# Two token blocks of a rational layer interleaved by units, with the first two units in halves

## The chip, the core and the metric

The kernel runs on one core of a Trainium2 chip. The metric is the device time of one execution in microseconds (us). Its engines are TensorE (PE in the rows, with its weight loads as PEld), VectorE (DVE), ScalarE (ACT), GpSimd (POOL) and SyncE (SP), which issues most transfers.

## What is computed

Three layers on 3072 tokens (4 batches x 768) of width 384:

```python
y = attn(q, k, v, a_re, a_im)             # linear attention by a complex decaying state
x = y.transpose(0, 2, 1, 3).reshape(3072, 384)
h = x @ w_in                              # 384 -> 2048
P = a[0] + a[1]*h + a[2]*h*h + a[3]*h*h*h
Q = 1.0 + abs(b[0])*abs(h) + abs(b[1])*h*h
x = (P / (Q + 1e-06)) @ w_out             # 2048 -> 384
# routed layer: the best of 8 experts for each token, times its gate
out[mask] = gate_w[mask, None] * (relu(x[mask] @ w1[e]) @ w2[e])
```

All matrices are fp32.

## The kernel before

**Stages.** The recurrence takes the first 250 us or so; the rational layer lies from 254 to about 690 us, the routed layer from there to 930, then the last rows are scattered.

**The rational layer.** Tokens are cut into 8 blocks of 384, the 2048 hidden columns into 8 units of 256, two halves of 128. `unit(b, i)` does unit `i` of block `b`. Each fp32 operand is a high part rounded to fp32r plus the rest (`xh`, `xl`, `wi..0`, `wi..1`, `wo..0`, `wo..1`, `gh`, `gl`), and each product is three matmuls: high x high, low x high, high x low. So a unit has 18 matmuls on `w_in` (`mm1`, L1016, 9 for each half), into PSUM tile `ph0` or `ph1` (two banks each, one for each half), and 18 on `w_out` (`mm2`, L1061), into three accumulators of one bank, one for each 128 tokens, that run over all 8 units of the block. Between them lies the rational function: on ScalarE Abs (L1039), Square (L1040), a second Square of h (L1042), Ln (L1045), Exp (L1046) and the cast to `gh` (L1050), on VectorE four SCALAR_TENSOR_TENSOR (L1044, L1047 to L1049) and the low part `gl` (L1051). Abs, the Square of L1042 and the VectorE operation of L1044 read h from PSUM, so `ph` is free again after these three. The accumulators and the h of unit 2 of block 0 (in halves, since both `ph` are taken then) come from a pool of four banks (`acc`). That unit writes its two halves to two of them.

**Parts.** The weights are loaded early as `wfi`, `wfo` and split late: the high cast on VectorE (L208), the low part on GpSimd (L210). `xsplit(b)` makes `xh` and `xl` of a block (L227, L231), two blocks in turn.

**The routed layer** goes over slots of 256 gathered tokens with the same `ph` and `acc` tiles (L1016 for the first product, L1458 for the second, transposes of gathered rows L1373, weight casts and splits L1411, `gl` L1447). Small blocks for the rest of the tokens lie beside the later slots: their rows are gathered by GpSimd, transposed (L1545), multiplied by weights `mw` (L1560, L1570) and their results turned (L1564, L1578).

**The order of the work.** No queue is written out by hand. Every piece of work is handed to a `Plan` with its engine or engines, an assumed duration, what it reads and writes, and at times a due time. When the program is built, `Plan.emit` picks, piece by piece, the one that could start soonest by its own clock and is due first; `COST` and `LEAN` weigh the engines for pieces that two engines could take, `UNIT` and `GROUP` are the assumed times of a unit and a slot and set the due times with `LAG`, `RAMP`, `AHEAD`, `BEFORE` and `FETCH`. Each engine then runs its instructions in that fixed order, and waits come from the data.

Names of halves in the plan, as `("h", 2 * j + n)`, serve the plan alone. The waits in the program are set for the tiles that are allocated, `ph0` or `acc1`.

Of the kernel before, what the change touches and what calls it, by code (L numbers as in the profile page):

```python
# [9 lines left out]
F32 = mybir.dt.float32  # L10
# [109 lines left out]
def tile_recurrence_rational_moe(tc, q, k, v, a_re, a_im, w_in, w_out, ca, cb, emb, tau, w1, w2, cst_d, out):  # L120
    nc = tc.nc
    V, A, G, T, SY = nc.vector, nc.scalar, nc.gpsimd, nc.tensor, nc.sync

    with ExitStack() as top:
        top.enter_context(tc.manual_schedule())
        dram = top.enter_context(tc.tile_pool(name="dram", bufs=1, space=bass.MemoryType.DRAM))
        x2d = dram.tile([NT + 1, XC], F32, name="x2d")
        idl = [dram.tile([NID, 1], I32, name=f"idl{t}") for t in range(TPB)]
        safe = dram.tile([NT, WO], F32, name="safe")
        cp = top.enter_context(tc.tile_pool(name="cp", bufs=1))  # L130
        cst = cp.tile([P, C_N], F32, name="cst")

        def cc(o, n=1):
            return cst[:, o:o + n]

        def misc(i):
            return cc(C_MISC + i)

        ident = cc(C_ID, P)
        cnt = cp.tile([P, E], F32, name="cnt")  # L140
        V.memset(cnt, 0.0)

        with ExitStack() as run:
            xtp = run.enter_context(tc.tile_pool(name="xtp", bufs=1))
            xT = xtp.tile([P, KT, NT], F32, name="xT")
            wfp = run.enter_context(tc.tile_pool(name="wfp", bufs=1))
            hold = run.enter_context(tc.tile_pool(name="hold", bufs=1))
            parts = weight_parts(tc, hold, wfp)
            xs = input_parts(tc, hold, xT)
            bad = cp.tile([P, 3], I32, name="bad")  # L150
            coef = coefs(tc, ca, cb, tau, cp)

            def prepare(again):
                with ExitStack() as att:
                    attention(tc, att, q, k, v, a_re, a_im, w_in, w_out, emb, cst, cst_d, cc, misc, ident, hold, xT, bad, idl, x2d, coef, parts, xs, again)

            def layers(ctx, again):
                return mixture(tc, ctx, cst, cc, misc, ident, cp, hold, wfp, parts, xs, xT, cnt, idl, x2d, w1, w2, out, coef, bad, safe, again)

            prepare(False)  # L160
            with ExitStack() as first:
                rare, rest = layers(first, False)
                with tc.If(nc.values_load(rare, min_val=0, max_val=1) != 0):  # L163
                    rest()
            with tc.If(nc.values_load(bad[0:1, 0:1], min_val=0, max_val=1) != 0):
                xs.tiles.clear()
                prepare(True)
                sequential_attention(tc, q, k, v, a_re, a_im, cst, cc, ident, dram, xT, coef)
                for kk in range(KT):
                    xs.hi(nc.scalar, 0, kk)  # L170
                    xs.lo(nc.gpsimd, 0, kk)
                plain_rational(tc, coef, parts, xT, safe)
                with ExitStack() as second:
                    layers(second, True)[1]()

# [122 lines left out]

COST = {'A': 0.7094815, 'G': 0.3193946, 'V': 1.1, 'T': 0.0, 'S': 0.0}
LEAN = {'A': 0.1119026, 'G': 0.1802717, 'V': 0.4995443, 'T': 0.0, 'S': 0.0}  # L300
SPREAD = 0.0605191
EARLY_BY = -0.9788931
LEAN_FROM = 4.5359957
MOE = SimpleNamespace(price=COST, bias=LEAN, margin=EARLY_BY, start=LEAN_FROM, chain=0.0, warm=WINDOW, port=True, lat=0.13)
# [120 lines left out]
def attention(tc, ctx, q, k, v, a_re, a_im, w_in, w_out, emb, cst, cst_d, cc, misc, ident, hold, xT, bad, idl, x2d, coef, parts, xs, again):  # L425
# [511 lines left out]

def mixture(tc, ctx, cst, cc, misc, ident, cp, hold, wfp, parts, xs, xT, cnt, idl, x2d, w1, w2, out, coef, bad, safe, again):
    nc = tc.nc
# [3 lines left out]
    NQ = NF2 // 2  # L943
    UNIT, GROUP = 6.0000, 16.4000
    LAG = 6.0
    FIRST = 2
    DELAY = -0.4256865
    RAMP = 1.5
    LATER = 1.0
    AHEAD = 6.0  # L950
    BEFORE = 8.0
    FETCH = 0.0

# [15 lines left out]
    ub, ku = [*u, spared["gl3"]], [[("u", i)] for i in range(3)] + [[("gl", 3)]]  # L969
    hp = [ps.tile([P, 2, 512], F32, name=f"ph{i}") for i in range(2)]  # L970
    banks = [ps.tile([P, 512], F32, name=f"acc{i}") for i in range(4)]
    half = [hp[i][:, j, :] for j in range(2) for i in range(2)]
# [3 lines left out]
    add = lambda *a, due=1e9, **k: st.plan.add(*a, due=due + st.delay, **k)  # L976
    bank = lambda key: banks[st.plan.bank[key][1]]

    def copy(e, o, i):
        (A.copy if e == "A" else eng[e].tensor_copy)(o, i)  # L980
# [32 lines left out]
    def products(o, steps):  # L1013
        steps = list(steps)
        for n, (l, r) in enumerate(steps):
            T.matmul(o, l, r, start=(n == 0), stop=(n == len(steps) - 1))  # L1016

    def unit(b, i):
# [10 lines left out]
        due = UNIT * n + 2.94  # L1029
        if n == FIRST:  # L1030
            pieces = [(slice(j, j + 1), [("hu", j)], lambda j=j: bank(("hu", j))[:, :BLK].rearrange("p (o n) -> p o n", o=1)) for j in range(2)]
            for j in range(2):
                add(("T", 1.45), lambda e, j=j: mm1(bank(("hu", j))[:, :BLK], j), r=wkey("i", i) + xkey(b % 2), w=[("hu", j)], take=("C", ("hu", j)), due=due)
# [18 lines left out]
        for t in range(TPB):  # L1052
            key = ("acc", b, t)

            def mm2(e, t=t, key=key):
                o = bank(key)[:, :WO]
                sl = slice(t * P, (t + 1) * P)
                for j in range(2):
                    c = slice(j * WO, (j + 1) * WO)
                    for k, (x, y) in enumerate(((g, wh), (g, wl), (l, wh))):  # L1060
                        T.matmul(o, x[:, j, sl], y("o", i)[:, c], start=(i == 0 and j == 0 and k == 0), stop=(i == NP - 1 and j == 1 and k == 2))  # L1061

            add(("T", 0.98), mm2, r=kg + kl + wkey("o", i), w=[key], take=("C", key) if not i else None, due=UNIT * (n + LAG - max(4 - n, 0) * RAMP) + 0.997 * (t + 1))

# [11 lines left out]
    def route(b):  # L1076
# [16 lines left out]
        for t in range(TPB):  # L1093
            key = ("acc", b, t)
            add([("A", 0.46), ("V", 0.48)], lambda e, t=t, key=key: copy(e, spread()[t], bank(key)[:, :WO]), r=[key], w=[("row", t)] + over, give=key)
            if again:
                add(("S", 0.65), lambda e, t=t: SY.dma_start(rows[t], safe[b * BLK + t * P:b * BLK + (t + 1) * P, :]), w=[("row", t)], lat=1.8)
# [643 lines left out]
```

## Time and profile before

| | us |
|---|---|
| median of 3 runs | 949.84 (949.75 to 953.89) |
| the profiled execution | 952.94 |
| its span, first to last instruction | 951.2 |
| around the span | 1.7 |
| TensorE busy | 876.5 (92%) |
| VectorE busy | 738.4 (78%) |
| ScalarE busy | 704.6 (74%) |
| GpSimd busy | 239.5 (25%) |

The span is that of the one execution that was profiled, and the times in the rows below are from its start. Mean granted clock of TensorE over the span: 0.971 of 2.4 GHz. In a row of a timeline the number in brackets is the idle time of the engine just before the instruction, and what ended it.

### The profile page before, as it was taken

How to read it: one execution, taken by the hardware profiler on the slowest of the kernel's cores; microseconds unless marked ns; L12 is line 12 of the kernel's file. 1: busy time of each engine (PE TensorE's matmuls, PEld its weight loads, DVE VectorE, ACT ScalarE, POOL GpSimd, SP SyncE). 2: the span in 40 equal slices, each digit the busy share in tenths (PEclk: the TensorE clock that was granted, in tenths of full speed). 3: DMA queues.
4: the chain of work that ended last, by engine and by line, in shares of the span. 5: the costliest groups of instructions: out<-in, count | busy, mean ns of one | idle time of the engine just before them, and what ended most of it. 6: DMA issues, size and time to landing. Idle time of an engine off the chain costs nothing. (4 is left out here: it accounts for less than half of the span.)

```text
span 951.2 us, 16898 instructions
## 1 busy us (share of the span) xinstructions
PE 876.5 (92%) x6119; PEld 832.3 (88%) x6119; DVE 738.4 (78%) x1418; ACT 704.6 (74%) x1134; POOL 239.5 (25%) x184
## 2 busy tenths in 40 slices
PE   2999998989878999999999999999999979999991
PEld 2788987878778999999999999999999868889991
DVE  7989988989799879797978888796977875655610
ACT  7989998999586989888889888878653544555520
POOL 2425434546244110101000010102223143215400
PEclk9999999999889999999999999999999989999996
DMA  9987988784200000010100000123202166541500
GB/s 173 200 171 171 178 188 180 144 181 111 81 0 1 1 26 1 1 26 1 26 1 26 1 26 1 26 67 92 34 9 85 26 192 209 158 142 35 176 26 22
DMA packets 172873, 76.50 MB, mean 80 GB/s; under 512 B 140840, under 2 KB 167352, under 8 KB 172772
## 3 DMA queue, kind: packets, MB, share of 16 engines
q1 hardware_dynamic: 168804, 65.58, 30.5%
q0 software_dynamic: 3968, 9.66, 3.5%
q8 instruction: 52, 0.85, 0.4%
q14 instruction: 49, 0.40, 0.2%
HBM read 95.33 MB, written 9.96 MB: 111 GB/s over the span
## 5 line engine op out<-in xcount | busy, mean ns | idle before, releaser
L1016 PE MATMUL ph<-xh,wi 128*128 128x384 f32 (+1 forms) x1284 | 306.0, 317 | 8.4 <-DVE wfi L488 4.2
L1016 PEld LDWEIGHTS ph<-xh,wi 128*128 128x128 f32 x1284 | 223.7, 190 | 10.5 <-DVE wfi L488 4.4
L1061 PE MATMUL acc<-wo,gh 128*128 128x392 f32 x768 | 201.8, 344 | 4.1 <-ACT gh L1050 4.1
L1016 PE MATMUL ph<-xl,wi 128*128 128x384 f32 (+1 forms) x642 | 203.1, 316 | 0.0
L1061 PEld LDWEIGHTS acc<-wo,gh 128*128 128x128 f32 x768 | 141.1, 189 | 4.4 <-ACT gh L1050 4.4
L1061 PE MATMUL acc<-wo,gl 128*128 128x392 f32 x384 | 131.6, 343 | 2.5 <-DVE gl L1051 2.5
L1016 PEld LDWEIGHTS ph<-xl,wi 128*128 128x128 f32 x642 | 121.8, 190 | 0.0
L1124 POOL DMA_INDIRECT idl<-tok,pos x24 | 24.6, 1026 | 281.2 <-DVE pos L1121 177.4
L1061 PEld LDWEIGHTS acc<-wo,gl 128*128 128x128 f32 x384 | 72.6, 189 | 3.3 <-DVE gl L1051 3.3
L1458 PE MATMUL acc<-wo,gh 128*128 128x384 f32 x256 | 70.0, 355 | 3.4 <-DVE wo L1411 3.4
L1051 DVE TENSOR_TENSOR gl<-u,gh 128x768 fp32r<-128x768 f32 x48 | 47.0, 979 | 27.1 <-PE acc L1061 26.1
L1039 ACT ACTIVATE sq<-ph,quad 128x768 f32<-128x768 f32 x43 | 38.8, 902 | 30.2 <-PE ph L1016 27.3
L1446 ACT ACTIVATE gh<-ph 128x512 fp32r<-128x512 f32 x36 | 21.6, 599 | 48.7 <-PE ph L1016 33.4
L1415 POOL DMA_INDIRECT out_dram<-ah,ido x24 | 29.8, 1242 | 98.0 <-ACT ah L1463 54.9
L1458 PEld LDWEIGHTS acc<-wo,gh 128*128 128x128 f32 x256 | 45.8, 194 | 9.4 <-issue 4.9
L497 ACT COPY qkT<-bank 96x512 f32<-96x512 f32 x96 | 50.6, 586 | 2.0 <-PE bank L619 1.3
L628 PE MATMUL bank<-qkT 96*128 96x128 f32 x384 | 50.8, 280 | 1.2 <-ACT qkT L497 1.2
L1355 POOL DMA_INDIRECT xT<-x2d,ids x24 | 27.2, 1133 | 98.2 <-DVE oh L1102 45.9
L1044 DVE SCALAR_TENSOR_TENSOR u<-u,qtmp,ph 128x768 f32<-128x768 f32 x47 | 47.3, 1006 | 5.4 <-ACT u L1042 5.3
L618 PE MATMUL bank<-cst,qf 128*96 128x128 f32 x192 | 48.2, 290 | 3.2 <-ACT qkT L497 3.2
L628 PEld LDWEIGHTS bank<-qkT 96*128 96x128 f32 x384 | 47.0, 193 | 2.9 <-ACT qkT L497 2.7
L1047 DVE SCALAR_TENSOR_TENSOR sq<-sq,quad,ah 128x768 f32<-128x768 f32 x43 | 46.6, 1085 | 0.6 <-ACT ah L1046 0.5
(297 smaller groups left out, 2157.6 us busy)
## 6 DMA issues: line engine op xcount, KB each, us to landing
xT<-in_moe_w_dram SPq DMA_DIRECT2D x26, 1536.0 KB
mw<-in_moe_w_dram SPq DMA_DIRECT2D x32, 384.0 KB
raw<-in_moe_w_out_dram SPq DMA_DIRECT2D x16, 384.0 KB
raw<-in_moe_w_in_dram SPq DMA_DIRECT2D x16, 384.0 KB
x2d<-rows SPq DMA_DIRECT2D x24, 192.5 KB
a_re<-in_a_re_dram SPq DMA_DIRECT2D x24, 192.0 KB
a_im<-in_a_im_dram SPq DMA_DIRECT2D x24, 192.0 KB
k<-in_k_dram SPq DMA_DIRECT2D x24, 192.0 KB
```

The source lines that it names most:

```text
L497: (A.copy if e == "A" else eng[e].tensor_copy)(o, i)
L618: T.transpose(pv[:, i, 0, :], Q[:, 2 * j + i, :], ident)
L628: T.matmul(pb(b)[:, i * P:(i + 1) * P], O[:, i, 1, :], O[:, i, 0, :], start=True, stop=True)
L1016: T.matmul(o, l, r, start=(n == 0), stop=(n == len(steps) - 1))
L1039: add(("A", 0.81 if many else 0.45), lambda e, c=c, h=h: A.activation(z[:, c], h(), AF.Abs, scale=coef.kb), w=kh + kz_)
L1044: add(("V", 0.93 if many else 0.53), lambda e, c=c, h=h: V.scalar_tensor_tensor(out=w[:, c], in0=w[:, c], scalar=coef.d, in1=h(), op0=ALU. ...
L1047: add(("V", 0.93), lambda e: V.scalar_tensor_tensor(out=z, in0=z, scalar=coef.e, in1=s, op0=ALU.add, op1=ALU.mult), r=ks, w=kz_)
L1051: add(("V", 0.87), lambda e: V.tensor_tensor(out=l, in0=w, in1=g.bitcast(F32), op=ALU.subtract), r=kw + kg, w=kl, lat=0.27)
L1061: T.matmul(o, x[:, j, sl], y("o", i)[:, c], start=(i == 0 and j == 0 and k == 0), stop=(i == NP - 1 and j == 1 and k == 2))
L1355: G.indirect_dma_start(out=xg[i][t], out_offset=None, in_=x2d[0:n, :], in_offset=bass.IndirectOffsetOnAxis(ap=ids[i][:, t:t + 1], axis=0), ...
L1415: G.indirect_dma_start(out=out[:, :], out_offset=bass.IndirectOffsetOnAxis(ap=dst, axis=0), in_=src, in_offset=None, bounds_check=NT - 1, ...
L1458: T.matmul(o, x[:, j, sl], w[:, c], start=(q == 0 and j == 0 and n == 0), stop=(q == NQ - 1 and j == 1 and n == 2))
```

## The change

The units of blocks 0 and 1 are no longer done block after block. A list `PAIR` sets their order: units 0 to 2 of block 0, then a unit of block 1 and one of block 0 in turn, block 1 two units behind, then the rest of block 1. The units are counted along that list. The first two go through a new function `halves_of`, which does every step for each half of 128 columns by itself (L1032 for ScalarE and L1033 for VectorE in the changed program, casts L1043, `gl` L1044, matmuls on `w_out` L1051). Unit 2, and unit 16 of the list, hold h in two pool banks (`LOOSE`). Units 3 to 15 all hold h in the same tile, `ph0` (`hp[0]`), each half under a name of its own. Two blocks have six accumulators: four are pool banks, and two of block 1 lie in the two banks of the other `ph` (`AWAY`). Which bank pair is `ph` and which is the pool now follows the order in which the recurrence frees them (`order`); the second `ph` is named `ph2`, the pool banks `acc10`, `acc11`, `acc30`, `acc31`. `xsplit(1)` is handed in ahead of all units. The constants of the plan are other ones, for the whole of both layers.

```diff
-COST = {'A': 0.7094815, 'G': 0.3193946, 'V': 1.1, 'T': 0.0, 'S': 0.0}
+COST = {'A': 1.1052526, 'G': 0.0767626, 'V': 1.1, 'T': 0.0, 'S': 0.0}
...
+    free = [t for t, _ in sorted(plan.pools["B"], key=lambda x: x[1])]
+    return sorted(range(4), key=lambda p: max(free[2 * p:2 * p + 2]))
...
-    UNIT, GROUP = 6.0000, 16.4000
-    LAG = 6.0
-    FIRST = 2
+    UNIT, GROUP = 5.0768176, 13.3066269
+    LAG = 6.0000000
+    LOOSE = (2, 2 * NP)
+    SKEW = 2
+    PAIR = [x for i in range(NP + SKEW) for x in ((0, i), (1, i - SKEW)) if 0 <= x[1] < NP]
+    AWAY = {("acc", 1, 1): 1, ("acc", 1, 2): 3}
+    done = lambda b: PAIR.index((0, NP - 1)) + 1 if not b else NP * (b + 1)
...
-    hp = [ps.tile([P, 2, 512], F32, name=f"ph{i}") for i in range(2)]
-    banks = [ps.tile([P, 512], F32, name=f"acc{i}") for i in range(4)]
+    room = {p: [ps.tile([P, 512], F32, name=f"acc{p}{i}") for i in range(2)] if p in order[2:] else ps.tile([P, 2, 512], F32, name=f"ph{p}") for p in range(4)}
+    hp, banks = [room[p] for p in order[:2]], [t for p in order[2:] for t in room[p]]
...
+    def halves_of(b, i, n, mm1, tiles, keys):
+
+        r = [k for ks in keys for k in ks]
+        for j in range(2):
+            z, s, w, g, l = (t[:, j] for t in tiles)
+            h, kh = hp[n][:, j, :BLK], ("h", 2 * j + n)
...
+            act(0.45, z, h, AF.Abs, [kh], kz_, scale=coef.kb)
+            act(0.41, z, z, AF.Square, [], kz_, bias=coef.t)
+            act(0.5, w, h, AF.Square, [kh], kw, scale=coef.k, bias=coef.m)
+            dve(0.53, w, w, coef.d, h, ALU.add, ALU.mult, [kh], kw, False)
+            act(0.46, s, z, AF.Ln, kz_, ks, bias=coef.e)
+            act(0.41, s, s, AF.Exp, [], ks, scale=-1.0)
...
     def unit(b, i):
-        n = NP * b + i
-        o = (n - (n > FIRST)) % 2
+        n = PAIR.index((b, i)) if b < 2 else NP * b + i
+        paired = LOOSE[0] < n < LOOSE[1]
+        o = (n + (n > LOOSE[1])) % 2
...
-        if n == FIRST:
...
+        if n < LOOSE[0]:
+            halves_of(b, i, n, mm1, (z, s, w, g, l), (kz_, ks, kw, kg, kl))
+            return
...
+        elif paired:
+            pieces = [(slice(j, j + 1), [("h", 2 * j)], lambda j=j: hp[0][:, j:j + 1, :BLK]) for j in range(2)]
+            for j in range(2):
+                add(("T", 1.45), lambda e, j=j: mm1(hp[0][:, j, :BLK], j), r=wkey("i", i) + xkey(b % 2), w=[("h", 2 * j)], due=due)
...
+        if b < 2:
+            todo = PAIR[done(0) * b:done(b)]
+        else:
+            todo = [(b, i) for i in range(NP)]
+        for one in todo:
+            unit(*one)
```

Where the change moves instructions is seen in the order on an engine. First VectorE, from its last `wfi` of the recurrence on. Before (`u` and `sq` are working tiles of a unit, `seen` and `tok` tables of the routing):

```order
L488 SCALAR_TENSOR_TENSOR wfi_170<-wa_125,bank_151 128x384
L1073 MEMSET seen_2796 128x8
L1074 CAST tok<-cst 128x24
L208 CAST wi_0_2833<-wfi_162 128x2x384
L208 CAST wi_0_2838<-wfi_164 128x2x384
L208 CAST wo_0_2867<-wfo_161 128x784
L208 CAST wi_0_2869<-wfi_166 128x2x384
L1044 SCALAR_TENSOR_TENSOR u_2768<-u_2768,qtmp,ph_2779 128x768
L208 CAST wo_0_2883<-wfo_165 128x784
L208 CAST wi_0_2895<-wfi_168 128x2x384
L1047 SCALAR_TENSOR_TENSOR sq_2766<-sq_2766,quad,ah_2764 128x768
L1044 SCALAR_TENSOR_TENSOR u_2769<-u_2769,qtmp,ph_2780 128x768
```

And in the changed program, at the same place:

```order
L488 SCALAR_TENSOR_TENSOR wfi_170<-wa_125,bank_151 128x384
L1119 MEMSET seen_2796 128x8
L1120 CAST tok<-cst 128x24
L227 CAST xh_2824<-xT 128x384 x3
L231 TENSOR_TENSOR xl_2825<-xT,xh_2824 128x384 x3
L1033 SCALAR_TENSOR_TENSOR u_2768<-u_2768,qtmp,ph_2779 128x384
L208 CAST wo_0_2855<-wfo_161 128x784
L208 CAST wi_0_2858<-wfi_162 128x2x384
L208 CAST wi_0_2861<-wfi_164 128x2x384
L1033 SCALAR_TENSOR_TENSOR u_2768<-u_2768,qtmp,ph_2779 128x384
L1033 SCALAR_TENSOR_TENSOR sq_2766<-sq_2766,quad,ah_2764 128x384 x2
L1033 SCALAR_TENSOR_TENSOR sq_2766<-sq_2766,ah_2764 128x384 x2
```

The weight casts of block 0 (L208) made room for the split of block 1 (L227, L231), and the first unit's steps come in halves.

Second ScalarE, one unit of the middle of the first two blocks. Before, unit 5 of block 0, from its Abs to its Exp, and behind it the cast of unit 3 (`gl3s` to `gh`):

```order
L1039 ACTIVATE gh3s<-ph_2779,quad 128x768
L1042 ACTIVATE u_2769<-ph_2779,quad 128x768
L1040 ACTIVATE gh3s<-gh3s,quad 128x768
L1045 ACTIVATE gl2s<-gh3s,quad 128x768
L1046 ACTIVATE gl2s<-gl2s 128x768
L1050 CAST gh_2771<-gl3s 128x768
```

In the changed program a paired unit, with the `gh` cast of an earlier unit among its reads of `ph0`:

```order
L1084 ACTIVATE sq_2767<-ph_2779,quad 128x384
L1095 CAST gh_2773<-u_2769 128x768
L1087 ACTIVATE gl3s<-ph_2779,quad 128x384
L1084 ACTIVATE sq_2767<-ph_2779,quad 128x384
L1087 ACTIVATE gl3s<-ph_2779,quad 128x384
L1085 ACTIVATE sq_2767<-sq_2767,quad 128x768
L1090 ACTIVATE ah_2765<-sq_2767,quad 128x768
L1091 ACTIVATE ah_2765<-ah_2765 128x768
```

The reads of h are four halves in place of two whole ones, all from `ph0`, and a cast of another unit can stand between them.

Third TensorE, at the transpose of the small block's gathered rows (`rows`) in the routed layer. Before:

```order
L1016 MATMUL ph_2780<-xh_2619,wi_1_2503 128x256
L1373 MATMUL acc_2781<-cst,xT 128x128 x3
L1373 MATMUL acc_2783<-cst,xT 128x128 x3
L1373 MATMUL acc_2782<-cst,xT 128x128 x3
L1373 MATMUL acc_2784<-cst,xT 128x128 x3
L1545 MATMUL acc_2781<-cst,rows_3361 128x128 x3
L1458 MATMUL acc_2783<-wo_0_2883,gh_2771 128x384
```

In the changed program, where it is L1592, behind thirty matmuls on `w_out` of which the last stand here:

```order
L1505 MATMUL acc_2780<-wo_0_2183,gl2e 128x384
L1505 MATMUL acc_2780<-wo_0_2183,gh_2773 128x384
L1505 MATMUL acc_2780<-wo_1_2324,gh_2773 128x384
L1505 MATMUL acc_2780<-wo_0_2183,gl2e 128x384
L1592 MATMUL acc_2781<-cst,rows_3618 128x128 x3
L1505 MATMUL acc_2783<-wo_0_2183,gh_2773 128x384
```

The transpose moved from behind twelve other transposes (L1373) to behind the second products of a slot.

## Rows read from the trace of the kernel before

**Rows 1.** Page, part 1: busy us (share of the span) and instructions by engine.

```profile
PE 876.5 (92%) x6119; PEld 832.3 (88%) x6119; DVE 738.4 (78%) x1418; ACT 704.6 (74%) x1134; POOL 239.5 (25%) x184
```

**Rows 2.** Waits of TensorE, 245 to 660 us: us in total, times, longest.

```profile
PE ph L1016 <- DVE wfi L488: 4.2, 1, 4.2
PE acc L1061 <- ACT gh L1050: 4.1, 1, 4.1
PE ph L1016 <- DVE gl3s L1044: 1.9, 1, 1.9
PE ph L1016 <- POOL wi L210: 0.9, 1, 0.9
PE acc L1061 <- DVE gl L1051: 0.9, 1, 0.9
PE ph L1016 <- DVE u L1044: 0.7, 1, 0.7
```

**Rows 3.** Windows: length, busy of PE, PEld, DVE, ACT, POOL, clock, transfer share, GB/s.

```profile
250.00:275.00 25.00, 18.42 (x90) 17.79 (x90) 19.82 (x22) 15.61 (x22) 13.45 (x6) 0.86 0.08 21
275.00:300.00 25.00, 21.15 (x105) 20.31 (x106) 23.61 (x24) 17.30 (x21) 9.86 (x5) 0.86 0.00 1
300.00:325.00 25.00, 23.07 (x123) 22.75 (x122) 23.84 (x27) 23.66 (x31) 2.59 (x1) 0.93 0.00 1
325.00:650.00 325.00, 325.00 (x1851) 325.00 (x1851) 270.30 (x484) 281.15 (x395) 18.67 (x18) 1.00 0.09 22
```

**Rows 4.** Timeline of TensorE near 298 and 310: start, us, instruction.

```profile
298.32 0.51 PE L1016 MATMUL ph<-xh,wi 128*128 128x384 f32 x2
298.67 0.34 PE L1016 MATMUL ph<-xl,wi 128*128 128x384 f32 x1
...
309.88 0.52 PE L1016 MATMUL ph<-xl,wi 128*128 128x384 f32 x1
...
310.84 0.52 PE L1016 MATMUL ph<-xl,wi 128*128 128x384 f32 x1
```

**Rows 5.** Timeline of VectorE, 252 to 275 us.

```profile
253.23 0.55 DVE L488 SCALAR_TENSOR_TENSOR wfi<-wa,bank 128x384 f32<-128x384 f32 x1
258.69 0.18 DVE L1074 CAST tok<-cst 128x24 int32<-128x24 f32 x1 [4.91 <-DMA xT<-y]
...
259.76 2.22 DVE L208 CAST wo<-wfo 128x784 fp32r<-128x784 f32 x1
...
264.96 0.56 DVE L208 CAST wo<-wfo 128x784 fp32r<-128x784 f32 x1
```

**Rows 6.** Timeline of ScalarE, 251 to 280 us.

```profile
268.18 0.58 ACT L1039 ACTIVATE gh3s<-acc,quad 128x384 f32<-128x384 f32 x1
268.65 0.68 ACT L1042 ACTIVATE u<-acc,quad 128x384 f32<-128x384 f32 x1
...
276.14 0.83 ACT L1050 CAST gh<-u 128x768 fp32r<-128x768 f32 x1 [4.60 <-DVE u L1049]
```

**Rows 7.** VectorE by line and shape, 250 to 330 us: busy us, mean ns.

```profile
L1044 DVE SCALAR_TENSOR_TENSOR u<-u,qtmp,acc 128x384 f32<-128x384 f32 x2 | 1.1, 601 | 0.0
```

**Rows 8.** Waits of TensorE, 640 to 951 us.

```profile
PE acc L1545 <- DMA rows<-x2d,hids: 3.9, 1, 3.9
PE acc L1458 <- DVE wo L1411: 3.4, 1, 3.4
PE acc L1373 <- ACT xh L980: 1.9, 1, 1.9
PE acc L1061 <- DVE gl L1051: 1.6, 1, 1.6
...
PE ph L1578 <- ACT gh3e L1446: 0.4, 1, 0.4
```

**Rows 9.** Windows around the two longest late waits, columns as in rows 3.

```profile
700.00:725.00 25.00, 21.58 (x146) 21.29 (x145) 18.23 (x65) 9.06 (x16) 7.40 (x7) 0.93 0.14 33
775.00:800.00 25.00, 21.14 (x142) 16.71 (x141) 16.83 (x34) 11.56 (x20) 8.58 (x6) 0.86 0.69 215
```

More of the change, by code (lines that the diff above doesn't have):

```diff
@@ L154, in prepare, with layers @@
                 with ExitStack() as att:
[L155 to L160, printed above, removed]
+                    return attention(tc, att, q, k, v, a_re, a_im, w_in, w_out, emb, cst, cst_d, cc, misc, ident, hold, xT, bad, idl, x2d, coef, parts, xs, again)
+            def layers(ctx, again, order):
+                return mixture(tc, ctx, order, cst, cc, misc, ident, cp, hold, wfp, parts, xs, xT, cnt, idl, x2d, w1, w2, out, coef, bad, safe, again)
+            order = prepare(False)
             with ExitStack() as first:
-                rare, rest = layers(first, False)
+                rare, rest = layers(first, False, order)
                 with tc.If(nc.values_load(rare, min_val=0, max_val=1) != 0):
@@ L173, in tile_recurrence_rational_moe @@
                 with ExitStack() as second:
-                    layers(second, True)[1]()
+                    layers(second, True, order)[1]()
 HOLD = ("s2", "ws", "re0", "im0", "re1", "im1", "s10", "th", "tl", "s11")
@@ L935, in plain_rational, with mixture @@
                 SY.dma_start(safe[b * BLK + t * P:b * BLK + (t + 1) * P, :], y)
-def mixture(tc, ctx, cst, cc, misc, ident, cp, hold, wfp, parts, xs, xT, cnt, idl, x2d, w1, w2, out, coef, bad, safe, again):
+def mixture(tc, ctx, order, cst, cc, misc, ident, cp, hold, wfp, parts, xs, xT, cnt, idl, x2d, w1, w2, out, coef, bad, safe, again):
     nc = tc.nc
@@ L976, in mixture @@
     add = lambda *a, due=1e9, **k: st.plan.add(*a, due=due + st.delay, **k)
-    bank = lambda key: banks[st.plan.bank[key][1]]
+    bank = lambda key: half[AWAY[key]] if key in AWAY else banks[st.plan.bank[key][1]]
     def copy(e, o, i):
@@ L1016, in products, with mm2 @@
             T.matmul(o, l, r, start=(n == 0), stop=(n == len(steps) - 1))
+    def halves_of(b, i, n, mm1, tiles, keys):
[3 more added lines that the diff above has]
+            h, kh = hp[n][:, j, :BLK], ("h", 2 * j + n)
+            kz_, ks, kw, kg, kl = ([("half", n, j, x)] for x in range(5))
+            add(("T", 1.45), lambda e, j=j, h=h: mm1(h, j), r=wkey("i", i) + xkey(b % 2), w=[kh])
+            act = lambda d, o, x, f, k, w, **kw: add(("A", d), lambda e: A.activation(o, x, f, **kw), r=k + r, w=w)
+            dve = lambda d, o, a, c, x, p, q, k, w, port=True: add(("V", d), lambda e: V.scalar_tensor_tensor(out=o, in0=a, scalar=c, in1=x, op0=p, op1=q), r=k + r, w=w, port=port)
+            act(0.45, z, h, AF.Abs, [kh], kz_, scale=coef.kb)
[4 more added lines that the diff above has]
+            act(0.41, s, s, AF.Exp, [], ks, scale=-1.0)
+            dve(0.5, z, z, coef.e, s, ALU.add, ALU.mult, ks, kz_)
+            dve(0.47, z, z, 2.0, s, ALU.subtract, ALU.mult, ks, kz_)
+            dve(0.5, w, w, coef.nc0, z, ALU.add, ALU.mult, kz_, kw)
+            add(("A", 0.4), lambda e, g=g, w=w: A.copy(g, w), r=kw + r, w=kg)
+            add(("V", 0.47), lambda e, g=g, l=l, w=w: V.tensor_tensor(out=l, in0=w, in1=g.bitcast(F32), op=ALU.subtract), r=kw + kg + r, w=kl, lat=0.27)
+            for t in range(TPB):
+                key = ("acc", b, t)
+                def mm2(e, j=j, t=t, key=key, g=g, l=l):
+                    o, c, sl = bank(key)[:, :WO], slice(j * WO, (j + 1) * WO), slice(t * P, (t + 1) * P)
+                    for k, (x, y) in enumerate(((g, wh), (g, wl), (l, wh))):
+                        T.matmul(o, x[:, sl], y("o", i)[:, c], start=(i == 0 and j == 0 and k == 0), stop=False)
+                add(("T", 0.49), mm2, r=kg + kl + wkey("o", i) + r, w=[key], take=("C", key) if not i and not j else None, due=UNIT * n + 8.0)
@@ L1029, in unit @@
         due = UNIT * n + 2.94
-        if n == FIRST:
-            pieces = [(slice(j, j + 1), [("hu", j)], lambda j=j: bank(("hu", j))[:, :BLK].rearrange("p (o n) -> p o n", o=1)) for j in range(2)]
-            for j in range(2):
-                add(("T", 1.45), lambda e, j=j: mm1(bank(("hu", j))[:, :BLK], j), r=wkey("i", i) + xkey(b % 2), w=[("hu", j)], take=("C", ("hu", j)), due=due)
+        if n < LOOSE[0]:
+            halves_of(b, i, n, mm1, (z, s, w, g, l), (kz_, ks, kw, kg, kl))
+            return
+        if n in LOOSE:
+            pieces = [(slice(j, j + 1), [("hu", n, j)], lambda j=j: bank(("hu", n, j))[:, :BLK].rearrange("p (o n) -> p o n", o=1)) for j in range(2)]
+            for j in range(2):
+                add(("T", 1.45), lambda e, j=j: mm1(bank(("hu", n, j))[:, :BLK], j), r=wkey("i", i) + xkey(b % 2), w=[("hu", n, j)], take=("C", ("hu", n, j)), due=due)
+        elif paired:
+            pieces = [(slice(j, j + 1), [("h", 2 * j)], lambda j=j: hp[0][:, j:j + 1, :BLK]) for j in range(2)]
+            for j in range(2):
+                add(("T", 1.45), lambda e, j=j: mm1(hp[0][:, j, :BLK], j), r=wkey("i", i) + xkey(b % 2), w=[("h", 2 * j)], due=due)
         else:
@@ L1061, in mm2 @@
                         T.matmul(o, x[:, j, sl], y("o", i)[:, c], start=(i == 0 and j == 0 and k == 0), stop=(i == NP - 1 and j == 1 and k == 2))
-            add(("T", 0.98), mm2, r=kg + kl + wkey("o", i), w=[key], take=("C", key) if not i else None, due=UNIT * (n + LAG - max(4 - n, 0) * RAMP) + 0.997 * (t + 1))
+            away = [("h", AWAY[key])] if key in AWAY else []
+            add(("T", 0.98), mm2, r=kg + kl + wkey("o", i), w=[key] + away, take=("C", key) if not i and not away else None, due=UNIT * (n + LAG - max(4 - n, 0) * RAMP) + 0.997 * (t + 1))
     ET = [mybir.EngineType.SP]
@@ L1094, in route @@
             key = ("acc", b, t)
-            add([("A", 0.46), ("V", 0.48)], lambda e, t=t, key=key: copy(e, spread()[t], bank(key)[:, :WO]), r=[key], w=[("row", t)] + over, give=key)
+            away = [("h", AWAY[key])] if key in AWAY else []
+            add([("A", 0.46), ("V", 0.48)], lambda e, t=t, key=key: copy(e, spread()[t], bank(key)[:, :WO]), r=[key] + away, w=[("row", t)] + over, give=None if away else key)
             if again:
@@ L1114, in count @@
             T.matmul(o[:, TPB * E:(TPB + 1) * E], cc(C_ONE, P), then[:, 0, :], start=True, stop=True)
-        add(("T", 0.31), count, r=["oh", kn, kt], w=[pc], take=("C", pc), due=UNIT * NP * (b + 1) + (6.0 if last else 30.0))
+        add(("T", 0.31), count, r=["oh", kn, kt], w=[pc], take=("C", pc), due=UNIT * done(b) + (6.0 if last else 30.0))
         rop(lambda: V.tensor_copy(cnt, bank(pc)[:, TPB * E:(TPB + 1) * E]), r=[pc], w=["cnt"])
@@ L1129, in route @@
         for t in range(TPB):
-            add(("G", 1.04), lambda e, t=t: scatter(e, t), r=["pos"], w=[("idl", t)], lat=6.5, due=UNIT * NP * (b + 1) + (14.0 if last else 40.0))
+            add(("G", 1.04), lambda e, t=t: scatter(e, t), r=["pos"], w=[("idl", t)], lat=6.5, due=UNIT * done(b) + (14.0 if last else 40.0))
         for t in range(TPB):
@@ L1148, in route @@
             vop(lambda t=t: V.reciprocal(rows[t][:, DM:XC], sm[:, t:t + 1]), r=["sm", "lg"], w=[("row", t)])
-            add(("S", 0.65), lambda e, t=t: SY.dma_start(x2d[b * BLK + t * P:b * BLK + (t + 1) * P, :], rows[t][:, :XC]), r=[("row", t)], w=[("x2d", b, t)], lat=1.8, dma=0.55, due=UNIT * NP * (b + 1) + 46.0)
+            add(("S", 0.65), lambda e, t=t: SY.dma_start(x2d[b * BLK + t * P:b * BLK + (t + 1) * P, :], rows[t][:, :XC]), r=[("row", t)], w=[("x2d", b, t)], lat=1.8, dma=0.55, due=UNIT * done(b) + 46.0)
     sp = ctx.enter_context(tc.tile_pool(name="e_s", bufs=1))
@@ L1597, in mixture @@
         split(n)
+    xsplit(1)
     for b in range(NBLK):
-        if b + 1 < NBLK:
+        if 0 < b < NBLK - 1:
             xsplit(b + 1)
@@ L1609, in mixture @@
             gather(2)
-        for i in range(NP):
-            unit(b, i)
+        if b < 2:
[4 more added lines that the diff above has]
+            unit(*one)
         route(b)
```

16 lines of the change are left out of this document (8 added, 8 removed).

## The prediction

> **What bounds the kernel now.** I read the page first: TensorE is busy 92% of the span [rows 1], so time is won only where it stands idle or runs slowly, and lost wherever the change makes it wait. The busy time by windows shows where that is [rows 3]: from 325 to 650 us the matmuls fill 325.00 of 325.00 us at clock 1.00, while between 250 and 325 they fill 18.42, 21.15 and 23.07 us of each 25, at clocks of 0.86, 0.86 and 0.93. The chain of waits of TensorE from 245 to 660 us names six waits and no other [rows 2]: 4.2 us before the first matmul of the rational layer, 4.1 before the first matmul on `w_out`, then 1.9, 0.9, 0.9 and 0.7. After the first, 8.5 us are left. To them comes the slow clock: at 309.88 to 310.84 three matmuls take 0.96 us, 0.32 each, against 0.35 us for two, 0.175 each, at 298.32 [rows 4]. That is 1.2 GHz against 2.4. About nine matmuls after 277 and ten after 309 went at the slow step, some 2.8 us lost. So the stage from 253.84 to 325 us loses 8.5 + 2.8 = 11.3 us, and this is all that an interleaved opening can win apart from the first wait. Later, from 640 us on, eight waits sum to 13.8 us, the two largest 3.9 and 3.4 us [rows 8], with clocks of 0.86 and 0.93 in their windows [rows 9].
>
> **The first wait, 4.2 us: cost 0.** The banks are now handed out in the order in which the recurrence frees them. But the wait is for the last `wfi` on VectorE, which starts at 253.23 and takes 0.55 [rows 2, 5]; the matmul that starts the layer in the changed program stands behind that same row, and the slow clock behind it stays. If the ordering did release it, 4.2 us would be gained; I put that among the rivals.
>
> **The first matmul on `w_out`.** TensorE has 72 matmuls ahead of it instead of 90, so it arrives earlier: from 253.84, 14 at the slow step (4.6 us) and 58 at 0.175 (10.1), about 268.6 us. What must be ready is `gh` of unit 0. VectorE starts at 258.69 in both programs, since it waits for the transfers of y [rows 5]. The first order block shows what now stands ahead of unit 0 there: the six split instructions of block 1 (about 2.4 us, an estimate: three of half the 0.56 us cast, with three `xl` of about 0.5), then a half, three casts (1.6 us), a half. Six more half instructions (3.2 us, from 601 ns for a half [rows 7]) end unit 0 near 268 us if nothing stretches them. Splits on GpSimd do stretch: the same `wo` cast took 2.22 us beside one and 0.56 without [rows 5]. Three splits stand early instead of six; with one to three stretches of 1.4 us the first `gh` half comes at 269 to 272. So this wait is 0.5 to 3.5 us; I take 2.5 (it was 4.1). For the next wait I take 1.2 instead of 0.9, for the slow clock behind them 1.4 as now, and 1.0 for the waits behind splits that are left of 0.9, 1.9 and 0.7. Together 6.1 us.
>
> **The paired stage, 13 units.** This is the term that decides. Before, the rational units alternate between `ph0` and `ph1`, so that a unit's first products may be written while the other tile is still read. After, units 3 to 15 all write `ph0`, since `ph2` holds accumulators of block 1. Its two halves have names of their own in the planner, but in the built program the first Abs waits for all 18 matmuls and the next unit's first matmul for VectorE's second half. What lies between: two Abs and two Square halves on ScalarE, with steps of 0.47 (268.18 to 268.65, for an Abs that lasts 0.58) and, with the same overlap of 0.11, about 0.57 for a Square of 0.68, the last counted whole [rows 6], 2.2 us; a VectorE half, 0.60 [rows 7]; the tail of the last matmul and three handovers, together 0.3 (an estimate, from ends and starts in these rows). That is 3.1 us, and 3.8 where a `gh` cast stands between them (0.83 less the overlap [rows 6]; the second order block shows it), and more when ScalarE is still busy with an instruction of 0.9 us as the products end. What covers it is mostly one unit's 18 matmuls on `w_out`, 18 x 0.178 = 3.2 us. The wait per unit lies between 0 and 1.4 us. I take 0.9, nearest to the single such waits that before shows (0.7, 0.9, 0.9 [rows 2]): 13 x 0.9 = 11.7 us, in a stretch in which TensorE now never waits.
>
> Here the Trainium skill bears. The rows of before show no wait at all from 325 to 650 us [rows 3], with two tiles in turn; by that alone the paired stage would cost 0. The page "Perfetto Trace Analysis", section "Matmuls", says that independent groups should go round different PSUM banks, so that emptying one lies under the next group's matmuls. This change gives that up for 13 units, and by the page each unit would show what its emptying has over the other matmuls, the 0 to 1.4 us above; no run here shows it yet.
>
> Opening and paired stage: 6.1 + 11.7 - 11.3 = **+6.5 us**.
>
> **The rest of the rational layer** has the same units with new due times and TensorE saturated: 0. Its cover is full buffers ahead of TensorE, and the one wait there, near its end, is 1.6 us [rows 8].
>
> **The routed layer.** The constants order it anew. The small block's transpose waits 3.9 us for gathered rows [rows 8]; twelve transposes stand right ahead of it, and afterwards thirty matmuls on `w_out` do (third order block shows the last). Thirty at 0.175 are 5.2 us, which covers 3.9. With about half of the up to 3.5 us that a clock of 0.86 costs over 25 us [rows 9] this gives back up to 6. The 3.4 us wait for a `wo` cast may go too, with up to 1.8 us of slow clock: the far end is about -11. New waits are as possible; the nearest are the 1.9 and 1.6 us of now [rows 8]. Below nothing, too, because one more wait of 3.4 us would eat the gain. I take -6 + 1.5 = **-4.5 us**, ends -11 and +3. The drain after the last matmul is untouched.
>
> Sum: +6.5 - 4.5 = +2 us. The profiled execution took 952.94 us, 3.1 above the median of the three; on it the sum is 955, on the median 949.84 it is **952 us**.
>
> **Rivals.**
> *The paired stage holds TensorE full (faster).* Were the chains hidden, 11.7 us fall away: -5.2 in the opening, -4.5 later, 940 us. For it: ScalarE and VectorE have 13 to 17% to spare there (281 and 270 of 325 us busy [rows 3]). Against: 3.1 to 3.8 us stand against 3.2 of cover. It decides from a wait per unit under about 0.3 us.
> *Nothing comes back late (slower).* The stage loses its 6.5 and the routed layer gains 0, or a wait per unit is 1.4 (+6.5 more): 956 to 963 us. For it: an order that starts later meets the same transfers.
> *The slow clock returns in the paired stage (slower).* After the 1.9 us wait the step was 0.32, after the 0.9 us one at 297.7 it stayed 0.175 [rows 2, 4]. If thirteen short waits bring the clock of the window 300 to 325, 0.93 [rows 3], over some 90 us, that is 6 us more, 958. By the page "TensorE: Matmul & The Clock Gate", section "HAM oscillation", repeated idle gaps send the array back to its slow state each time; the row with 0.9 us does not agree for so short a gap.
> *The bank order does release the first matmul.* -4.2, 948 us. Against: the waited row is the same.
> *The routed layer gains its far end.* -11 + 6.5, 945 us.
>
> **How the numbers follow.** Chances: the forecast (948 to 955) 0.40, nothing back or the long wait 0.26, slow clock 0.07, hidden stage 0.17, early start 0.04, far end late 0.06. 0.5%, 4.75 us, is about what a measurement of this kernel can tell from no change, so faster means below 945.1 and slower above 954.6. Faster has the hidden stage and most of the far end, 0.23; slower the two slower rivals and the upper edge of the forecast, 0.37; same 0.40. The range 942 to 962 leaves the hidden stage's centre out below and the longest waits above. The forecast's own range is 948 to 955.
>
> **What the profile after would show.** First matmul at 253.8 behind the same `wfi`. First `w_out` matmul at 269 to 272. Between about 285 and 375 us some ten waits of TensorE of 0.4 to 1.4 us, each for a half on `ph0` or for `gl`, at clock 1.00. The same matmul of block 2 some 6 us later than before. The transpose of gathered rows without its 3.9 us. It is wrong if the paired stage shows 25.00 in 25, if the clock is below 0.95 there, or if the routed layer's waits sum to over 14 us.

## The result, and the profile after

Twenty executions of the changed kernel have a median of 960.99 us (955.7 to 965.57), twenty of the kernel before, run beside them, 954.82 (949.75 to 961.05). The ratio is 1.0069, with a 95% interval of 1.0053 to 1.0084: slower by 0.7%, some 6.6 us. Of the three runs that stood ahead of the prediction two were the lowest of the twenty. The profiled execution of the changed kernel took 956.77 us with a span of 954.6, 4.2 us below its median; that of the kernel before, 952.94, lies 1.9 below its own.

The waits of TensorE from 245 to 645 us in the changed kernel, where [rows 2] had six (us in total, times, longest):

```profile
PE ph L1022 <- DVE u L1089: 8.6, 10, 1.8
PE ph L1022 <- DVE wfi L488: 4.2, 1, 4.2
PE acc L1051 <- DVE u L1089: 3.3, 1, 3.3
PE acc L1106 <- DVE gl L1096: 2.4, 5, 0.6
PE acc L1051 <- ACT gh L1043: 2.3, 1, 2.3
PE ph L1022 <- DVE gl3s L1089: 1.2, 2, 1.0
PE ph L1022 <- DVE u L1033: 0.6, 1, 0.6
PE acc L1051 <- DVE gl L1044: 0.4, 1, 0.4
```

Without the first wait, the same 4.2 us in both, they sum to 18.8 us in 21 waits, against 8.5 in five. The first, fourth and sixth line are the paired stage: 12.2 us, most of them a first product (L1022) that may not be written into `ph0` before VectorE (L1089) has read it. The windows, columns as in [rows 3]:

```profile
250.00:275.00 25.00, 17.11 (x84) 15.82 (x84) 17.46 (x33) 15.22 (x29) 5.92 (x3) 0.93 0.06 15
275.00:300.00 25.00, 21.65 (x112) 21.01 (x113) 21.67 (x28) 18.92 (x28) 7.90 (x4) 0.93 0.00 1
300.00:325.00 25.00, 21.51 (x114) 19.45 (x112) 18.63 (x23) 18.05 (x27) 10.39 (x4) 1.00 0.00 1
325.00:350.00 25.00, 21.83 (x116) 19.74 (x115) 18.36 (x23) 19.18 (x29) 2.54 (x1) 1.00 0.00 1
350.00:375.00 25.00, 21.79 (x117) 20.02 (x116) 18.84 (x32) 17.76 (x30) 0.00 (x0) 1.00 0.00 0
375.00:400.00 25.00, 25.00 (x145) 25.00 (x144) 21.36 (x54) 22.09 (x36) 3.63 (x3) 1.00 0.07 24
```

From 300 to 375 us 114 to 117 matmuls run in 25 us, where 145 do when nothing waits; VectorE, ScalarE and TensorE all have idle time at once, as in a loop in which each waits for the other. The clock is 1.00 there. Late, [rows 8] had eight waits with 13.8 us; now there are 8.6 us:

```profile
PE ph L1022 <- DVE gl L1494: 3.9, 2, 3.4
PE acc L1505 <- DVE gl L1494: 1.6, 2, 1.1
PE ph L1611 <- ACT sq L1620: 1.2, 2, 0.7
PE acc L1420 <- DMA xT<-x2d,ids: 0.8, 1, 0.8
PE ph L1022 <- DVE xl L1425: 0.6, 1, 0.6
PE acc L1420 <- DVE ex L1165: 0.5, 1, 0.5
```

The wait for gathered rows (3.9) and the one for a `wo` cast (3.4) are gone. Two marks on TensorE cut the program in two, whatever the order in between: its first product of the routed layer (the first one 256 wide), and its last matmul. In the timelines they stand at 684.41 and 934.23 us here, at 675.13 and 930.38 before. With the first matmul at 252.00 here and 253.84 before, the rational layer took 432.4 us instead of 421.3, **11.1 more**, and the routed layer 249.8 instead of 255.3, **5.4 less**. (Before the first mark the changed kernel has done three transposes fewer among some 2300 matmuls, 0.3 us.)

### The profile page after: what moved, and what is told of

Read it like the earlier page. It is cut to its first block, busy times and chain, and to the rows that moved or that the text cites. A ratio compares the mean times of both kernels' runs of the same rounds, so it can differ in the third digit from the quotient of the medians.

```text
span 954.6 us, 16965 instructions
## 1 busy us (share of the span) xinstructions
PE 874.9 (92%) x6119; PEld 825.3 (86%) x6119; DVE 743.6 (78%) x1469; ACT 702.5 (74%) x1150; POOL 233.1 (24%) x181
## 5 line engine op out<-in xcount | busy, mean ns | idle before, releaser
L1022 PE MATMUL ph<-xh,wi 128*128 128x384 f32 (+1 forms) x1272 | 304.3, 317 | 18.7 <-DVE u L1089 8.6
L1022 PEld LDWEIGHTS ph<-xh,wi 128*128 128x128 f32 x1272 | 221.2, 190 | 25.3 <-DVE u L1089 12.8
L1022 PE MATMUL ph<-xl,wi 128*128 128x384 f32 (+1 forms) x636 | 200.9, 316 | 0.6 <-DVE xl L1425 0.6
L1106 PE MATMUL acc<-wo,gh 128*128 128x392 f32 x680 | 177.4, 342 | 0.0
L1106 PEld LDWEIGHTS acc<-wo,gh 128*128 128x128 f32 x680 | 123.7, 188 | 0.0
L1022 PEld LDWEIGHTS ph<-xl,wi 128*128 128x128 f32 x636 | 120.7, 190 | 0.9 <-DVE xl L1425 0.9
L1106 PE MATMUL acc<-wo,gl 128*128 128x392 f32 x340 | 116.3, 342 | 2.4 <-DVE gl L1096 2.4
L1505 PE MATMUL acc<-wo,gh 128*128 128x384 f32 x256 | 67.6, 344 | 0.1
L1106 PEld LDWEIGHTS acc<-wo,gl 128*128 128x128 f32 x340 | 63.8, 188 | 4.3 <-DVE gl L1096 4.3
L1084 ACT ACTIVATE sq<-ph,quad 128x768 f32<-128x768 f32 (+1 forms) x49 | 38.5, 786 | 36.6 <-PE ph L1022 32.2
L1089 DVE SCALAR_TENSOR_TENSOR u<-u,qtmp,ph 128x768 f32<-128x768 f32 (+1 forms) x53 | 45.9, 873 | 20.6 <-ACT u L1087 17.3
L1505 PEld LDWEIGHTS acc<-wo,gh 128*128 128x128 f32 x256 | 44.5, 188 | 4.3 <-issue 4.3
L1087 ACT ACTIVATE u<-ph,quad 128x768 f32<-128x768 f32 (+1 forms) x53 | 46.7, 881 | 1.1 <-DVE gl L1096 1.1
```

What stands on the lines that cost most here:

```text
L1084: add(("A", 0.81 if many else 0.45), lambda e, c=c, h=h: A.activation(z[:, c], h(), AF.Abs, scale=coef.kb), w=kh + kz_)
L1087: add(("A", 0.9 if many else 0.5), lambda e, c=c, h=h: A.activation(w[:, c], h(), AF.Square, scale=coef.k, bias=coef.m), w=kh + kw)
L1505: T.matmul(o, x[:, j, sl], w[:, c], start=(q == 0 and j == 0 and n == 0), stop=(q == NQ - 1 and j == 1 and n == 2))
```

## The experiments

Times are medians; ratios are those to the kernel before, run on the same chip. The two parts are cut at the marks above.

**E1. Two tiles for the paired h.** The order on each engine is that of the changed kernel.

```diff
+    early = ExitStack()
+    ep = early.enter_context(tc.tile_pool(name="m_pe", bufs=1, space=PSUM))
+    pz = [ep.tile([P, 512], F32, name=f"phz{j}") for j in range(2)]
...
-            h, kh = hp[n][:, j, :BLK], ("h", 2 * j + n)
+            h, kh = (hp[n][:, j, :BLK] if n else pz[j][:, :BLK]), ("h", 2 * j + n)
...
-            pieces = [(slice(j, j + 1), [("h", 2 * j)], lambda j=j: hp[0][:, j:j + 1, :BLK]) for j in range(2)]
+            pieces = [(slice(j, j + 1), [("h", 2 * j)], lambda j=j: pz[j][:, :BLK].rearrange("p (o n) -> p o n", o=1)) for j in range(2)]
```

The later units get the whole tile of two banks in the same place, once the paired units are through.

> The changed kernel, except that the h of units 0 and 3 to 15 lies in two PSUM tiles of one bank each instead of one tile of two banks; the order on every engine stays, only what is waited for changes. Theory A (the waits of the paired stage, 12.2 us in the profile of the changed kernel, come from both halves of h being one tile, so that the first Abs waits for all 18 matmuls and the next products for the last half that is read): these waits fall to 4 us or less, and the time falls by 8 to 11 us, to 950 to 953, below the kernel before. Theory B (they come from the interleaved order itself, the casts between the reads and the chain from h to gl): the waits stay at 9 us or more and the time stays within 3 us of the changed kernel's 961.

Measured: 946.81 us, ratio 0.9921 (0.9896 to 0.9947), 14 us below the changed kernel. The waits from 245 to 645 us:

```profile
PE phz L1040 <- DVE wfi L488: 4.2, 1, 4.2
PE acc L1124 <- DVE gl L1114: 2.5, 3, 2.1
PE acc L1069 <- DVE u L1107: 2.2, 1, 2.2
PE acc L1069 <- ACT gh L1061: 2.0, 1, 2.0
PE acc L1069 <- DVE gl L1062: 0.4, 1, 0.4
```

No first product waits for a read of h any more; of the 12.2 us of the paired stage 2.5 are left. The first Abs of a unit shows the cause directly: in the changed kernel that of one unit starts at 300.69 us, behind the last of the unit's 18 matmuls (300.32), in E1 that of the same unit starts at 298.93, while the second nine of the 18 run (to 300.13). Theory A holds and theory B falls. The time lies 3 us below the 950 to 953 that theory A gave: the gain is more than the 9.7 us of listed waits that went from this stage.

**E2. The kernel before with the new constants alone.**

```diff
-COST = {'A': 0.7094815, 'G': 0.3193946, 'V': 1.1, 'T': 0.0, 'S': 0.0}
+COST = {'A': 1.1052526, 'G': 0.0767626, 'V': 1.1, 'T': 0.0, 'S': 0.0}
...
-    UNIT, GROUP = 6.0000, 16.4000
+    UNIT, GROUP = 5.0768176, 13.3066269
```

> The kernel before with nothing but the constants of the changed plan (COST, LEAN, SPREAD, LEAN_FROM, UNIT, GROUP, RAMP, AHEAD, BEFORE, FETCH). Theory C (the 6 us that the changed kernel wins back between the last rational units and the end come from the constants): the waits of TensorE from 640 us on fall from 13.8 to 9 or less, and the time is 5 to 11 us under the kernel before, 944 to 950. Theory D (they come back because the changed kernel reaches the routed layer 10 us later, with its weights and rows already there): the late waits stay at 12 or more and the time is within 2 us of the kernel before.

Measured: 943.94 us, ratio 0.9885 (0.9858 to 0.9912). Late waits:

```profile
PE ph L1016 <- DVE gl L1447: 3.8, 2, 3.3
PE acc L1458 <- DVE gl L1447: 1.7, 2, 1.2
PE ph L1564 <- ACT sq L1573: 1.2, 2, 0.7
```

with the same three small ones behind them as in the changed kernel. The late order is the constants' doing: theory C. Of what the two parts gain, 9.5 us, more than half lies late (the routed layer takes 249.96 us); the rest is in the rational layer (417.1 us instead of 421.3), where the wait of 1.9 shrank to 0.9, two others by 0.2 each, and the clock from 300 to 325 us was 1.00.

**E3. The changed kernel with the constants of before**, the same edit the other way round.

> The changed kernel with the constants of the plan before. Theory C: the late gain is lost, the time is 6 to 11 us over the changed kernel, 967 to 972. Theory D: within 3 us of the changed kernel. On both the waits of the paired stage stay near 12 us.

Measured: 964.04 us, ratio 1.0108 (1.0082 to 1.0134), only 3 us over the changed kernel. The late gain is lost as theory C has it: the routed layer takes 255.2 us, 5.4 more, and the rational layer, 431.9, hardly changes. The medians still lie only 3 us apart where 6 to 11 were expected. The profiled executions, 964.52 and 956.77, are 7.8 apart, but that of the changed kernel is the one 4.2 us below its median.

**E4. Bank pairs in another order.**

```diff
-            order = prepare(False)
+            prepare(False)
+            order = [1, 0, 2, 3]
```

> The changed kernel with the bank pairs handed out as 1, 0, 2, 3, so that the first unit's h lies in the pair that the last work on the recurrence's banks uses. If the wait before the first matmul of the rational layer hangs on which bank is free (the purpose of the ordering), it grows past 4.2 us or the first matmul starts later; if it hangs on the last work of the whole recurrence, as I read it, it stays at 4.1 to 4.3 us and the rest of the profile stays the same.

One execution, 957.77 us. Its first matmul of the rational layer, on TensorE's timeline:

```profile
251.45 0.69 PE L1023 MATMUL ph<-xh,wi 128*128 128x384 f32 x1 [4.18 <-DVE wfi L489]
```

4.18 us and the same releaser. Which of these two bank pairs comes first decides nothing. The wait is also the same with two tiles (E1) and before; that it is for the end of the work on all the recurrence's banks fits this, and no run tests it by itself.

**E5. Two tiles, constants of before.** E1 and E3 together: the interleave alone.

> The interleave alone, rightly waited for: the changed kernel with two tiles for the paired h, as in the first run of the experiments, and with the constants of the plan before. If the interleave with halves is worth something by itself (its purpose: fewer and shorter waits in the opening), this is 2 us or more below the kernel before. If all that the split version won over the kernel before came from the constants, it lies within 2 us of the kernel before, 953 to 957. Its paired stage shows waits of 4 us or less.

Measured: 950.31 us, ratio 0.9952 (0.9926 to 0.9978), about 4 us below the kernel before. Its rational layer takes 419.0 us, 2.3 less than before, its routed layer 254.0. So the interleave has a worth of its own, of a few microseconds, once its waits are right. The paired stage's waits on h and `gl` are 2.2 us.

**E6. New constants and halves, no interleave.** E2 with `halves_of` taken over from the changed kernel for the first two units:

```diff
+        if n < FIRST:
+            halves_of(b, i, n, mm1, (z, s, w, g, l), (kz_, ks, kw, kg, kl))
+            return
         if n == FIRST:
```

> The kernel before with the new constants and, on top, the first two units of block 0 in halves; no interleave, both ph tiles in turn. Theory E (the halves shorten the way to the first matmul on w_out, 4.1 us of waiting without them, 2.3 with them in the changed kernel): that wait falls below 3 us and the time is 1 to 2 us below that of the new constants alone (943.9). Rival: the time comes out the same, since VectorE's later casts and GpSimd's splits then end later, and the wait for them takes its place.

Measured: 943.14 us, ratio 0.9864 (0.9822 to 0.9906), not told apart from E2. The waits after the first:

```profile
PE acc L1095 <- ACT gh L1084: 2.0, 1, 2.0
PE ph L1016 <- ACT ah L1026: 2.0, 1, 2.0
PE ph L1016 <- DVE gl3s L1078: 0.8, 2, 0.6
PE acc L1095 <- DVE gl L1085: 0.7, 1, 0.7
PE ph L1016 <- DVE u L1078: 0.5, 1, 0.5
```

The 4.1 us wait (at 277.1 in E2) is gone, but a first product waits 2.0 us at 267.9 and a product on `w_out` 2.0 at 295.8, at places where E2 has no wait above 0.9 us. The halves moved the wait, as the rival has it, though to other places than it named.

**E7. E2 with RAMP at 2.8.**

```diff
-    RAMP = 1.8988600
+    RAMP = 2.8
```

> The kernel before with the new constants and RAMP at 2.8 instead of 1.9, so that the first units' matmuls on w_out are due earlier and get ahead of later units' first products. If the waits of the opening are a matter of this order, those after the first w_out matmul (0.9, 0.9, 0.7, 0.5 us with RAMP 1.9) fall together by 1 us or more, and the time is 1 to 3 us below 943.9; otherwise it is the same within 1 us.

Measured: 941.34 us, ratio 0.9847 (0.9803 to 0.989). It is the fastest of all and beats both kernels, but its interval overlaps E2's, so the step from E2 to it is not shown. The waits after the first on `w_out` went from 3.0 to 2.3 us, less than expected.

**E8, E9, E10. Two more profiled executions of the changed kernel, one more of the kernel before.**

> The changed kernel unchanged, for a second profiled execution: the first one took 956.8 us at a mean clock of 0.982, while its twenty executions have a median of 961.0 and most of them a mean clock of 0.971 to 0.976. Theory F (what a usual execution has more than the profiled one is slow clock in the opening and the paired stage, after waits that left the clock alone in the first profile): with a mean clock of 0.976 or less, the windows from 250 to 400 us show a clock below 0.93 in two or more of six, with the same waits within 1 us. Rival: the clock of these windows is as in the first profile (0.93, 0.93, 1.00 from then on) and the difference lies in the recurrence or late.

> The same kernel once more, a third profiled execution; the same numbers as for the one before are expected of each theory.

> The kernel before unchanged, a second profiled execution. Its first had clocks of 0.86, 0.86 and 0.93 in the windows from 250 to 325 us and 1.00 from 325 to 650. With few waits in that stage, the clocks should repeat within 0.07 in each window, and the waits of TensorE within 0.5 us.

955.44, 955.79 and 953.40 us. Windows of E8 and then of E9:

```profile
250.00:275.00 25.00, 18.93 (x84) 17.94 (x84) 17.34 (x33) 14.57 (x29) 5.94 (x3) 0.81 0.07 18
275.00:300.00 25.00, 19.39 (x104) 17.96 (x103) 21.64 (x29) 19.93 (x31) 7.52 (x3) 0.98 0.00 1
300.00:325.00 25.00, 21.40 (x105) 19.55 (x105) 17.43 (x23) 16.41 (x24) 8.26 (x3) 0.93 0.00 1
325.00:375.00 50.00, 43.62 (x232) 39.83 (x231) 36.76 (x48) 36.08 (x54) 5.00 (x2) 1.00 0.00 1
```

```profile
250.00:275.00 25.00, 18.46 (x87) 17.61 (x84) 17.34 (x35) 14.33 (x27) 5.95 (x3) 0.83 0.10 28
275.00:300.00 25.00, 21.18 (x101) 20.02 (x100) 21.35 (x30) 20.14 (x31) 7.56 (x3) 0.83 0.00 1
300.00:325.00 25.00, 21.40 (x106) 19.56 (x105) 17.46 (x23) 16.88 (x25) 8.26 (x3) 0.93 0.00 1
325.00:375.00 50.00, 43.63 (x231) 39.82 (x230) 37.29 (x49) 35.26 (x53) 4.98 (x2) 1.00 0.00 1
```

Theory F is not borne out. E9 has two windows below 0.93, as it asked, E8 one, the first profile none; from 325 to 375 us the clock is 1.00 in all three. But both have the mean clock of a usual execution, 0.976, and both took some 5 us less than the median of 961.0, so the slow clock alone is not what a usual one has more. The rational layer took 433.9 us in both (first matmul at 253.58 and 254.37, first routed product at 687.48 and 688.28) against 432.4 in the first profile and 421.3 in E10. The routed layer took 244.6 and 244.7 us, since the 3.4 us wait at 780 us did not occur in them; with E1, E2, E4 and E6 it did. Why it comes and goes is open. An estimate from these parts: the first profile, with its 3.4 us wait, would take 960.6 us if it started as late as E9 (2.4 us) and had its rational layer (1.5 us); no execution with all three was profiled. E10 repeats the waits of [rows 2] within 0.1 us and the clocks of [rows 3]; only late does it differ, where the transpose of gathered rows waited 5.0 us in place of 3.9, and the wait of 1.9 us for `xh` [rows 8] is missing.

| | rational layer, us | routed layer, us | ratio to before |
|---|---|---|---|
| before | 421.3 | 255.3 | 1 |
| changed | 432.4 | 249.8 | 1.0069 |
| E1 two tiles | 420.6 | 249.8 | 0.9921 |
| E2 new constants alone | 417.1 | 250.0 | 0.9885 |
| E3 changed, old constants | 431.9 | 255.2 | 1.0108 |
| E5 two tiles, old constants | 419.0 | 254.0 | 0.9952 |

## Why the prediction was right, and where its sizes were off

The time fell into the range, on the side that the prediction gave 0.37, and outside the likeliest case's own 948 to 955. The mechanisms were the ones named; two prices were too small, that of the second wait on `w_out` and that of a wait as such. Of the 9 us between the forecast of 952 and 961, 5 are no error of the mechanism at all: the forecast stood on 949.84, the median of three runs, where twenty have 954.82. The change itself was put at +2 us and measured at 6 to 7. With both errors on the same side the range held the time by 1 us, which is luck.

*First wait, cost 0.* Right: 4.18 us in the changed kernel and in E4.

*First matmul on `w_out`: 2.5, then 1.2.* The first is right, 2.33 us. The second was mis-sized: 0.36 for `gl` and then 3.35 us. That wait names VectorE's read of h in unit 2 (L1089): the third accumulator shares a pool bank with a half of that unit's h, and the prediction had not looked at who holds the banks. It was 2.2 and 2.4 us in E8 and E9. The 1.0 for waits behind splits was 0.6, and that one is for VectorE's read of a half (L1033).

*Paired stage, 13 x 0.9 = 11.7 us.* Right in cause and nearly in what the view lists: 12.2 us, in 17 waits of 0.2 to 1.8 us where some ten of 0.4 to 1.4 were expected. E1 shows the cause: the same order with the two halves as two tiles has 2.5 us. By "Perfetto Trace Analysis", section "Matmuls", in the Trainium skill, matmul groups should go round PSUM banks so that one is emptied under the next. The halves lay in two banks already; it was the tile, not the bank, that the waits were set for. E1 agrees with the page once banks and tiles coincide.

*The price of a wait* is where the sum failed. A listed wait counts from the modelled end of the last matmul to the next start. In the changed kernel:

```profile
295.79 0.34 PE L1106 MATMUL ph<-wo,gl 128*128 128x392 f32 x1
297.24 0.45 PE L1022 MATMUL ph<-xh,wi 128*128 128x384 f32 x1 [1.11 <-DVE u L1089]
297.52 0.34 PE L1022 MATMUL ph<-xl,wi 128*128 128x384 f32 x1
297.70 0.51 PE L1022 MATMUL ph<-xh,wi 128*128 128x384 f32 x2
```

Unhindered, the second would start 0.175 after the first; it starts 1.45 after, 1.27 lost for 1.11 listed, and the third another 0.28 behind instead of 0.175. So this wait costs 0.27 us more than it lists, in pipelining lost before and after. Over the whole rational layer, behind its first matmul, it is much the same. The listed waits grew by 9.2 us, from six to 22: 10.3 as above, less 1.1 for a wait near the end (1.6 before [rows 8], 0.5 now). The steps between starts of matmuls, against unhindered steps of 0.175 and 0.179 us, lost another 4.0 us across these waits and just behind them, 0.25 for each of the sixteen more. Against that, 24 matmuls went at the step of 0.32 us where 34 did before, 1.7 us less, and three transposes fewer are 0.3: 9.2 + 4.0 - 1.7 - 0.3 = 11.2, and the layer took 11.1 more. In E8 and E9, with more slow matmuls, it took 12.6 more. The prediction's +6.5 for this part took 11.7 as the whole price of thirteen waits.

*The routed layer, -4.5.* Right: -5.4, and about -10 in E8 and E9, near the far end of -11. There the two misses nearly cancel: +12.6 and -10 come out where +6.5 and -4.5 do, at some +2 us. The wait for gathered rows went as argued, behind the thirty matmuls. E2 shows that the constants alone do it. In E3 and E5, interleaved with the old constants, that wait is gone too, but others of up to 2.2 us stand in its place, and little of the gain is left: 255.2 and 254.0 us.

*Rivals.* The slow clock hardly came to the paired stage: from 285 to 375 us the clock was 1.00 in the first profile and 0.98 in E8 and E9. In those two it fell once, right behind a wait of 1.8 us near 306 us; the same wait at 304.1 left it alone in the first profile, and from 325 us on, with waits of 1.0 us at most, it was 1.00 in all three. "TensorE: Matmul & The Clock Gate", section "HAM oscillation", in the Trainium skill, has idle gaps throw the array back to its slow state; its case has longer gaps, and the waits of 1.0 us and less here did not do it. The hidden stage and the early start did not come. The long wait per unit came nearest, in effect: 12.2 us in 17 waits are 0.94 listed per unit, and with 0.27 for each wait about 1.3 paid.

What stays open: with the new constants the interleave gains nothing (E1 lies 3 us above E2, though their intervals overlap a little), with the old ones about 4 (E5). The waits of E1 and E2 in the opening are alike, 7.1 us each without the first, and E1's clocks are lower in its profile, 0.82, 0.84 and 0.93 from 250 to 325 us against 0.86, 0.86 and 1.00. In these two profiles that is the difference: 48 matmuls of E1's rational layer went at the slow step and 26 of E2's, which is 3.2 us of the 3.4 between them. One profile each doesn't settle whether it is so in every execution. Nor is it shown where a usual execution of the changed kernel spends the rest: in the profiles it is 2 to 4 us slower than before, by the medians of twenty 6.

## What to carry to other kernels

A planner that gives the halves of a buffer names of their own gains nothing if the program sets its waits for the whole buffer: check which instruction each wait in the built program names, and make the tile as small as the piece that is handed over. Here that one step, at the same order, was worth 14 us. When a change brings a structure and new tuning constants together, time the constants alone; here they were worth 11 us in the old structure, and hid some ten of the 17 us that the new structure loses against them (changed kernel against E2). Price a new wait with what it takes from the pipelining before and after it (here 0.25 us each), not with its idle time alone.

## What the runs showed of the hardware

The time of one execution varies by some 10 us over twenty, and part of that arises ahead of the change. The first matmul of the rational layer started between 251.45 and 258.18 us after the span's start in the twelve profiled executions, which have the same matmuls in the same order up to there, and always behind the same wait of 4.2 us. From there to the routed layer the two executions of the kernel before took 421.3 us each, the three of the changed kernel 432.4, 433.9 and 433.9. Parts of a program that are cut at fixed matmuls can be compared more sharply than whole times.
